# Retention and two gated MLP layers on one core: dense products of the first weight blocks dealt over the units of retention in another way

## Chip, core and metric

One core of a Trainium2 chip runs the whole kernel. The metric is the device time of one execution in microseconds, as the median of several runs. The profile is one execution with the hardware profiler on.

## What is computed

Retention over 2 x 8 heads (sequence 768, head size 64), then two MLP layers on its output x (1536 tokens by 512), all in fp32:

```python
state = gamma * state + einsum('bhd,bhe->bhde', k[:, :, t], v[:, :, t])
y[:, :, t] = scale * einsum('bhd,bhde->bhe', q[:, :, t], state)
...
x = ((x @ w_a) * (x @ w_b)) @ moe_w_out        # 512 -> 1536 -> 512
h = x @ w_in                                   # 512 -> 2048
y = np.maximum(0.01 * h, h) @ moe2_w_out       # 2048 -> 512
```

## The kernel before

**Precision.** TensorE runs the dense products in fp32r. Each fp32 operand is split in a high part (a ScalarE copy that rounds, names ending in h) and a low part (source minus high part, on VectorE, names ending in l), and a product is three matmuls: high by high, high by low, low by high (`mm3`, L256 to L258). Weights come from HBM as 64-bit words (`raw_...`, L286). For each block three ScalarE instructions take the word apart (`begin_steps`, L307, L309, L311) and three VectorE instructions round it (`round_steps`: L325, L327 and L329); then `high` (L944) and `low` (L950) split it.

**Retention** comes first. The 1536 tokens are 3 tiles of 512 and the 8 heads 4 pairs: 12 units (tile by tile, 4 pairs in each), driven by the loop over `u` at L1005. Units 0 to 3 use chunks of 128 tokens, units 4 to 11 short chunks of 64. For a short-chunk unit TensorE makes the states (`kv`, from scaled keys `kd` and `v`), the scores (`sc`), the part within a chunk (`x` from `P` and `v`) and the part across chunks (`x` from `qs` and the running states `cr`, `ca`). In iteration u it issues states(u+1) between within(u), then scores(u+1) between across(u), all at L644. The other engines then serve the next iteration:

- VectorE: seven or eight updates of the running state (`adds`, L606 and L608), `P` of unit u+1 (`masked`, L650), the low part of x (L251), and rounding and low parts of weights;
- ScalarE: scaled keys (L583), the high part of x (L250), plain or negated copies of x (`xf`, L663 and L665), the weights' first steps and high parts;
- GpSimd: scaled queries `qs` of later units (L588), each when its `q` has landed, and later its own DMAs.

Every engine works through its instructions in the program's order. The tiles are held in a pool of 83 slots of SBUF; a new tile waits for what last used its slot. PSUM has 8 banks, one for each of kv, sc, x and each open dense product.

**The dense products of blocks 0 and 1** of the first layer (a and b, three tiles of x: 48 steps of three 512-column matmuls) fill TensorE between the small products. The generator `first_blocks` (L953) lists them, and the loop takes `FILL[u]` steps at the end of iteration u, the rest after the last unit (L1089). A name such as pa01 or h01 has the tile first and the block second; tile n of the loop is stored under TURN[n]. `ROUND` says in which units a block is rounded (`weigh`): a and b of block 0 in units 3 and 4, those of block 1 in units 5 to 8, in two parts each. `PUMP[u]` takes items from a queue, among them block 2's rounding (from u = 8).

**After retention**, blocks 2 to 11 run in a scheme that needs fewer products but sums of x's quarters. The sums (`outer`, L1077) are eight accumulating DMAs on `xf` from GpSimd's queue, two in each of units 8 to 11; each half of them is a chain of four, in which one waits for the landing of the one before. `mixed_items` then splits eight of these sums into high and low parts (L760, L763), four queue items in each of units 9 to 11. Block 2's first matmul is `pa` from x10h and a2h.

```python
for _ in range(FILL.get(u, 0)):
    next(dense)
pump(PUMP.get(u, 0))
```

Of the kernel before, what the change touches and what calls it, by code (L numbers as in the profile page):

```python
# [10 lines left out]
F32R = mybir.dt.float32r  # L11
# [15 lines left out]
NPAIR = H // 2  # L27
# [8 lines left out]
NRAW = 4  # L36
NEXTRA = 10
NWARM = 10
FILL = {4: 4, 5: 4, 6: 4, 7: 4, 8: 4, 9: 4, 10: 4, 11: 4}
PUMP = {9: 0.6, 10: 0.6, 11: 0.6}  # L40
ROUND = {3: ("a", 0, 3), 4: ("b", 0, 3), 5: ("a", 1, 2), 6: ("a", 1, 1), 7: ("b", 1, 2), 8: ("b", 1, 1)}
NBLOCK = 2
AHEAD = 8
KEYS = {-1: (2,), 0: (3,), 3: (5,)}
QUERIES = {4: (6,), 5: (7, 8), 6: (9, 10), 7: (11,)}
CPT = TT // P
COUNT = {"a": FF1, "b": FF1, "wo": FF1, "wi": FF2, "wq": FF2}
HALF = FF2 // 2
# [180 lines left out]
def retention_moe_kernel(ctx: ExitStack, tc: tile.TileContext, ins, out):  # L229
# [14 lines left out]
    def as32(t):  # L244
        return t.bitcast(F32)

    def split(src, name, new=slots.new):

        hi, lo = new(F32R, name + "h"), new(F32R, name + "l")
        nc.scalar.copy(hi, src)  # L250
        nc.vector.tensor_sub(lo, src, as32(hi))  # L251
        return hi, lo
# [120 lines left out]
    def enqueue_split(key, keep=False, far=False):  # L373
        def high():
            weights[key] = slots.new(F32R, f"{key[0]}{key[1]}h"), slots.new(F32R, f"{key[0]}{key[1]}l")
            (nc.vector.tensor_copy if key[0] == "wi" and key[1] > 1 else nc.scalar.copy)(weights[key][0], rounded[key])

        def low():
            src = rounded.pop(key)
            if far:  # L380
                nc.scalar.mul(weights[key][1], as32(weights[key][0]), -1.0)
                nc.gpsimd.dma_start(weights[key][1], src, accum_op=ALU.add)
            else:
                nc.vector.tensor_sub(weights[key][1], src, as32(weights[key][0]))
            if keep:
                kept[key] = src
            else:
                slots.done(1)

        behind.extend([(0.05, high), (0.05 if far else 0.61, low)])  # L390

    def enqueue_next(f):
        for k in "ab":
            enqueue_round()
            enqueue_split((k, f), f in FAST, k == "a" and f in FAST[1:])

    kept = {}

# [160 lines left out]
    @known  # L559
    def wide_spreads(u, t, p, d):  # L560
        for h, r in enumerate(flip):
            nc.scalar.copy(spread[u % 2][r, 1:, heads[h]], broad[u % 2][r, 1:])
# [84 lines left out]
    @known  # L647
    def masked(u, t, p, d):
        d["P"] = slots.new(F32, f"P{u}")
        nc.vector.tensor_mul(by_sub(d["P"]), by_sub(d["sc"]), pair_table(p, 1))  # L650

    @known
    def leave_x(u, n, p, d):
        t = TURN[n]
        x[t, p] = split(d["x"], f"x{t}{p}")

    @known
    def copy_x(u, n, p, d):
        t = TURN[n]
        if t != 1:  # L660
            xf[t, p] = slots.new(F32, f"xf{t}{p}")
            if t:
                nc.scalar.mul(xf[t, p], d["x"], -1.0)  # L663
            else:
                nc.scalar.copy(xf[t, p], d["x"])  # L665
        slots.done(6)
        del un[u]
# [73 lines left out]

    S, yf, SY = {}, {}, {}

    def mixed_items(xf, S, name, summed=False):
        add, sub = nc.vector.tensor_add, nc.vector.tensor_sub
        for j in range(0 if summed else 2):
            for op, d, a, b in (
                (add, (2, 2 + j), (2, j), (2, 2 + j)),
                (sub, (2, j), (0, j), (2, j)),
                (sub, (0, j), (2, 2 + j), (0, j)),  # L750
                (sub, (0, 2 + j), (0, 2 + j), (0, j)),
            ):
                yield 0.61, lambda op=op, d=d, a=a, b=b: op(xf[d], xf[a], xf[b])
        for n, t, p in ((1, 2, 2), (3, 2, 0), (2, 0, 0), (4, 0, 2)):
            for j in range(2):
                key = (t, p + j)

                def high(n=n, key=key, j=j):
                    S[n, j] = slots.new(F32R, f"{name}{n}{j}h"), slots.new(F32R, f"{name}{n}{j}l")
                    nc.scalar.copy(S[n, j][0], xf[key])  # L760

                def low(n=n, key=key, j=j):
                    nc.vector.tensor_sub(S[n, j][1], xf.pop(key), as32(S[n, j][0]))  # L763
                    slots.done(1)

                yield 0.05, high
                yield 0.61, low
# [179 lines left out]
    def low():  # L947
        while lows:
            key = lows.pop()
            nc.vector.tensor_sub(weights[key][1], rounded.pop(key), as32(weights[key][0]))  # L950
            slots.done(1)

    def first_blocks():  # L953
        ps = {}
        all4 = range(KC)
        runs = [(0, 0, "a", all4), (0, 0, "b", all4)]
        runs += [(1, 0, k, kcs) for kcs in ((0, 1), (2,)) for k in "ab"] + [(0, 1, "a", (0, 1))]
        runs += [(1, 0, k, (3,)) for k in "ab"] + [(0, 1, "a", (2, 3)), (1, 1, "a", all4)]
        runs += [(n, 1, "b", all4) for n in range(2)]
        runs += [(2, f, k, all4) for f in range(2) for k in "ab"]  # L960
        for n, f, k, kcs in runs:
            t = TURN[n]
            for kc in kcs:
                if not kc:
                    ps[t, f, k] = bank(f"p{k}{t}{f}")
                ab_mm(ps[t, f, k], t, f, "ab".index(k), [kc])
                if kc == KC - 1 and k == "b":
                    ab_out(ps[t, f, "a"], ps[t, f, "b"], t, f)
                yield
# [4 lines left out]
    def keys(u):  # L974
        (wide_keys if u < NPAIR else scaled_keys)(u)

    def queries(u):
        (wide_queries if u < NPAIR else scaled_queries)(u)
# [5 lines left out]
    def rounding(u):  # L984
        weigh(u)
        if ROUND.get(u + 1, (0, 0, 0))[2] > 1:
            begin_weights()
        while done:
            high(done.pop())
# [15 lines left out]
    for u in range(-1, len(units)):  # L1005
        if u < NPAIR:
            if u < NPAIR - 1:
                wide_scores(u + 1)
            else:
                wide_within(u)  # L1010
                issue(states(u + 1))
                issue(scores(u + 1))
            if u < 0:
                keys(1)
                queries(1)
                keep_warm(3)
            if u == 0:
                wide_within(u)
            if u < NPAIR - 1:
                wide_states(u + 1)  # L1020
            else:
                masked(u + 1)
                for step in un[u + 1]["adds"]:
                    step()
            if u < 0:
                keep_warm(2)
            if 0 < u < NPAIR - 1:
                wide_within(u)
            wide_across(u)
            if u == NPAIR - 2:  # L1030
                keys(NPAIR)
                queries(NPAIR)
            leave_x(u)
            if u < NPAIR - 1:
                wide_spreads(u + 1)
            for v in KEYS.get(u, ()):
                keys(v)
                queries(v)
            copy_x(u)
            slots.tick()  # L1040
            rounding(u)
        else:
            issue(states(u + 1), within(u))
            issue(scores(u + 1), across(u))
            slots.tick()
            steps = un[u + 1]["adds"] if u + 1 in un else []
            low()
            for step in steps[:3]:
                step()
            masked(u + 1)  # L1050
            for step in steps[3:4]:
                step()
            keys(u + 2)
            for v in QUERIES.get(u, ()):
                queries(v)
            leave_x(u)
            for step in steps[4:]:
                step()
            rounding(u)
            copy_x(u)  # L1060
        for _ in range(FILL.get(u, 0)):
            next(dense)
        pump(PUMP.get(u, 0))
        loads(u + AHEAD)
        if u in (10, 11):
            load_weights()
        if u == 8:
            enqueue_next(2)
            queue.extend(behind)
            behind.clear()  # L1070
            queue.extend(sub_items(("a", 2), ("b", 2)))
        if u == 8:
            outer = [(xf[d], xf[a]) for d, a in outer]
        if u >= 8:
            for _ in range(2):
                d, a = outer.pop(0)
                nc.gpsimd.dma_start(d, a, accum_op=ALU.add)  # L1077
        if u == 8:
            spare.extend(mixed_items(xf, S, "s", True))
        for _ in range(4 if u > 8 else 0):  # L1080
            spare.pop(0)[1]()
        slots.tick()
    att.close()
# [437 lines left out]
```

## Time and profile before

| | us |
|---|---|
| median of 3 runs (lowest, highest) | 561.6 (561.35, 561.87) |
| the profiled execution | 561.61 |
| its span, first to last instruction | 559.8 |
| TensorE busy | 549.6 (98%) |
| VectorE busy | 461.5 (82%) |
| ScalarE busy | 385.4 (69%) |
| GpSimd busy | 154.9 (28%) |
| mean granted TensorE clock | 0.999 |

The profile calls TensorE PE, VectorE DVE, ScalarE ACT and GpSimd POOL. A row of the timeline has the start and the length of an instruction in us, the engine, the line, what is written from what, shapes, and in brackets how long the engine sat idle before it and what ended that. Matmuls overlap, and their ends are modelled: the distance between two starts says more than a length. Tile numbers are left out, so "pa<-x00h,a0h" is tile 0 and block 0.

### The profile page before, as it was taken

What the parts mean: (1) busy time and instruction counts of PE and PEld (TensorE: products, weight loads), DVE (VectorE), ACT (ScalarE), POOL (GpSimd) and SP (SyncE); (2) the same over time, 40 slices, a digit from 0 to 9 for tenths busy, and PEclk for the clock granted to TensorE, in tenths of its full rate; (3) what the DMA queues carried; (4) which work ended last, traced back from release to release, by engine and by line L of the source; (5) the groups of instructions that cost most, each with busy time, mean ns of one, the idle gap of its engine ahead of it and who ended that gap; (6) DMA issues with size and microseconds to landing.
All of it is one profiled execution on the core that took longest, in us unless ns stands there. A gap on an engine that the chain in (4) does not pass through costs nothing.

```text
span 559.8 us, 10494 instructions
## 1 busy us (share of the span) xinstructions
PE 549.6 (98%) x3745; PEld 462.3 (83%) x3745; DVE 461.5 (82%) x985; ACT 385.4 (69%) x795; POOL 154.9 (28%) x197
## 2 busy tenths in 40 slices
PE   9799999999999999999999999999999999999997
PEld 5777888888888888888888888888888888888886
DVE  5797887789998898999869878896977798999862
ACT  4864767678888888877757556778766886687800
POOL 2254101003213321267430130221333456600000
PEclk9999999999999999999999999999999999999999
DMA  8998614448887889699993361764777799964111
GB/s 316 395 385 232 151 42 117 127 119 228 238 233 206 249 229 299 200 326 232 247 218 96 58 131 42 213 179 151 227 239 224 209 274 241 224 163 118 57 57 57
DMA packets 49909, 108.52 MB, mean 194 GB/s; under 512 B 5952, under 2 KB 13376, under 8 KB 49856
## 3 DMA queue, kind: packets, MB, share of 16 engines
q1 hardware_dynamic: 27504, 66.86, 35.9%
q0 software_dynamic: 22064, 40.64, 34.0%
q8 instruction: 29, 0.48, 0.4%
q10 hardware_dynamic: 288, 0.34, 0.2%
q14 instruction: 24, 0.20, 0.1%
HBM read 74.00 MB, written 18.35 MB: 165 GB/s over the span
## 4 chain that ended last, share of the span: by engine, by line
PE 96%; DVE 2%; ACT 1%; issue 0%
PE blk L257 12%; PE blk L256 12%; PE blk L258 12%; PE top L257 5%; PE top L256 5%; PE top L258 5%; PE pa L256 4%; PE pb L258 4%; PE pb L256 4%; PE pb L257 4%; PE pa L257 4%; PE pa L258 4%; PE mid L256 3%; PE mid L257 3%; PE mid L258 3%; PE left L257 1%
## 5 line engine op out<-in xcount | busy, mean ns | idle before, releaser
L257 PE MATMUL blk<-form,form 128*128 128x512 f32 (+1 forms) x224 | 75.8, 339 | 0.0
L256 PE MATMUL blk<-form,form 128*128 128x512 f32 (+1 forms) x224 | 75.6, 337 | 0.0
L258 PE MATMUL blk<-form,form 128*128 128x512 f32 (+1 forms) x224 | 75.3, 336 | 0.0
L172 DVE TENSOR_TENSOR form<-g,form 128x512 fp32r<-128x512 f32 x112 | 57.5, 549 | 0.9
L257 PE MATMUL blk<-forma,forma 128*128 128x512 f32 (+1 forms) x168 | 56.9, 338 | 0.0
L256 PE MATMUL blk<-forma,forma 128*128 128x512 f32 (+1 forms) x168 | 56.7, 337 | 0.0
L258 PE MATMUL blk<-forma,forma 128*128 128x512 f32 (+1 forms) x168 | 56.4, 336 | 0.0
L166 ACT CAST form<-g 128x512 fp32r<-128x512 f32 x112 | 52.3, 511 | 5.1 <-DMA g<-g 3.2
L172 DVE TENSOR_TENSOR forma<-h,forma 128x512 fp32r<-128x512 f32 x84 | 43.0, 551 | 5.3 <-ACT forma L166 3.8
L256 PEld LDWEIGHTS blk<-form,form 128*128 128x128 f32 x224 | 42.5, 190 | 5.3
L257 PEld LDWEIGHTS blk<-form,form 128*128 128x128 f32 x224 | 42.5, 190 | 4.7
L258 PEld LDWEIGHTS blk<-form,form 128*128 128x128 f32 x224 | 42.3, 189 | 4.8
L166 ACT CAST forma<-h 128x512 fp32r<-128x512 f32 x84 | 38.8, 511 | 6.3 <-DMA h<-h 6.0
L717 POOL DMA_DIRECT2D farg<-g x26 | 15.6, 614 | 80.4 <-ACT g L1263 62.5
L145 POOL DMA_DIRECT2D h<-h x33 | 32.8, 1159 | 16.9 <-DVE h L847 5.1
L256 PEld LDWEIGHTS blk<-forma,forma 128*128 128x128 f32 x168 | 31.9, 190 | 4.0
L257 PEld LDWEIGHTS blk<-forma,forma 128*128 128x128 f32 x168 | 31.9, 190 | 3.6
L258 PEld LDWEIGHTS blk<-forma,forma 128*128 128x128 f32 x168 | 31.7, 189 | 3.6
L717 POOL DMA_DIRECT2D farh<-h x19 | 10.9, 575 | 75.4 <-DVE h L847 40.6
L172 DVE TENSOR_TENSOR form<-wq,form 128x256 fp32r<-128x256 f32 x56 | 23.3, 417 | 10.0 <-ACT form L166 9.9
L166 ACT CAST form<-wq 128x256 fp32r<-128x256 f32 x56 | 22.5, 402 | 6.4 <-PE blk L257 2.5
L145 POOL DMA_DIRECT2D g<-farg x22 | 22.0, 1046 | 7.9 <-DVE form L172 4.4
(3058 smaller groups left out, 1680.4 us busy)
## 6 DMA issues: line engine op xcount, KB each, us to landing
raw_wi<-in_w SPq DMA_DIRECT2D x16, 512.0 KB, 4.2
raw_wq<-in_w SPq DMA_DIRECT2D x16, 512.0 KB, 5.1
farg<-g POOLq DMA_DIRECT2D x26, 256.0 KB, 4.0
g<-farg SPq DMA_DIRECT2D x26, 256.0 KB, 6.7
raw_a<-in_wab SPq DMA_DIRECT2D x12, 512.0 KB, 5.0
raw_b<-in_wab SPq DMA_DIRECT2D x12, 512.0 KB, 5.0
raw_wo<-in_wo SPq DMA_DIRECT2D x12, 512.0 KB, 5.2
g<-farg POOLq DMA_DIRECT2D x20, 256.0 KB, 8.5
```

What stands on the lines that cost most here:

```text
L145: queue.append((0.0, lambda piece=piece: self.nc.gpsimd.dma_start(self.A(*d[1:], j)[piece], self.A(*x1[1:], j)[piece], accum_op=ALU.add)))
L166: nc.scalar.copy(h, src)
L172: nc.vector.tensor_sub(*todo.pop(0))
L256: nc.tensor.matmul(ps, w[0], x[0], start=first, stop=False, skip_group_check=more)
L257: nc.tensor.matmul(ps, w[0], x[1], start=False, stop=False, skip_group_check=more)
L258: nc.tensor.matmul(ps, w[1], x[0], start=False, stop=last, skip_group_check=more)
L717: nc.gpsimd.dma_start(self.far[t, f], self.tiles[t, f])
```

## The change

Steps are dealt as 4, then 6 in each of units 5 to 10, then 4, with 4 left after the last unit (before: 4 in each of units 4 to 11, 16 left). In `first_blocks` the products of block 0 with the second tile stay open over units 5 to 8, one quarter of x in each. Block 1's a and b are rounded in one unit each, 5 and 6. In units 3 and 4 rounding moves ahead of the state updates (unit 3) and of `P` (unit 4), and the high and low parts of a0 and b0 are made in that unit. Block 2's rounding and first sums are queued at u = 6 instead of 8, and PUMP takes them from u = 7. The low part of a2 and of the sums 3 and 4 (four tiles) is no longer a VectorE subtraction but a ScalarE multiplication by -1 and an accumulating DMA from GpSimd's queue. The eight `outer` sums are issued in units 8 and 9, four in each.

```diff
-FILL = {4: 4, 5: 4, 6: 4, 7: 4, 8: 4, 9: 4, 10: 4, 11: 4}
-PUMP = {9: 0.6, 10: 0.6, 11: 0.6}
-ROUND = {3: ("a", 0, 3), 4: ("b", 0, 3), 5: ("a", 1, 2), 6: ("a", 1, 1), 7: ("b", 1, 2), 8: ("b", 1, 1)}
+FILL = {4: 4, 5: 6, 6: 6, 7: 6, 8: 6, 9: 6, 10: 6, 11: 4}
+PUMP = {7: 1.2, 8: 1.6, 9: 1.2, 10: 1.2, 11: 1.2}
+ROUND = {3: ("a", 0, 3), 4: ("b", 0, 3), 5: ("a", 1, 3), 6: ("b", 1, 3)}
+LATER = {9: 4, 10: 6, 11: 6}
...
-            enqueue_split((k, f), f in FAST, k == "a" and f in FAST[1:])
+            enqueue_split((k, f), f in FAST, k == "a")
...
-                    nc.vector.tensor_sub(S[n, j][1], xf.pop(key), as32(S[n, j][0]))
+                    if n in far:
+                        nc.scalar.mul(S[n, j][1], as32(S[n, j][0]), -1.0)
+                        nc.gpsimd.dma_start(S[n, j][1], xf.pop(key), accum_op=ALU.add)
+                    else:
+                        nc.vector.tensor_sub(S[n, j][1], xf.pop(key), as32(S[n, j][0]))
...
                 masked(u + 1)
-                for step in un[u + 1]["adds"]:
+                weigh(u)
+                for step in un[u + 1]["adds"][:3]:
                     step()
...
+            if u == NPAIR - 1:
+                high(done.pop())
+                low()
+                for step in un[u + 1]["adds"][3:]:
+                    step()
+                x_low(u)
+                begin_weights()
...
+            if u == NPAIR:
+                weigh(u)
+                masked(u + 1)
+                for step in steps:
+                    step()
+                x_high(u)
+                keys(u + 2)
+                queries(u + 2)
+                high(done.pop())
+                low()
+                x_low(u)
+                begin_weights()
...
-        if u >= 8:
-            for _ in range(2):
+        if u in (8, 9):
+            for _ in range(4):
                 d, a = outer.pop(0)
                 nc.gpsimd.dma_start(d, a, accum_op=ALU.add)
         if u == 8:
-            spare.extend(mixed_items(xf, S, "s", True))
-        for _ in range(4 if u > 8 else 0):
+            spare.extend(mixed_items(xf, S, "s", True, (3, 4)))
+        for _ in range(min(LATER.get(u, 0), len(spare))):
```

**VectorE in iterations 3 and 4**, from the updates of unit 4 to b0's rounding, before. (cr0, cr1 and ca.. are running states, kv4 is unit 4's new states, sl the weight's low bits.)

```order
L251 TENSOR_TENSOR x03l_75_478<-x3_421,x03h_74_477 128x512
L325 TENSOR_SCALAR a0_68_408<-a0_68_408 128x512
L327 TENSOR_SCALAR a0_68_408<-a0_68_408 128x512
L329 ISA a0_68_408<-a0_68_408,sl0_409 128x1024
L950 TENSOR_TENSOR a0l_81_498<-a0_68_408,a0h_80_497 128x512
L608 SCALAR_TENSOR_TENSOR cr1_86<-ca11_80,second_76,kv5_508 128x64
L608 SCALAR_TENSOR_TENSOR cr1_86<-cr1_86,second_76,kv5_508 128x64 x2
L650 TENSOR_TENSOR P5_86_575<-sc5_540,second_76 128x512
L606 COPY cr1_86<-kv5_508 128x64
L251 TENSOR_TENSOR x20l_90_583<-x4_509,x20h_89_582 128x512
L608 SCALAR_TENSOR_TENSOR cr1_86<-cr1_86,second_76,kv5_508 128x64 x2
L608 SCALAR_TENSOR_TENSOR ca10_79<-cr1_86,second_76,kv5_508 128x64
```

And now:

```order
L965 TENSOR_TENSOR a0l_79_486<-a0_68_408,a0h_78_485 128x512
L607 COPY cr0_85<-kv4_430 128x64
L609 SCALAR_TENSOR_TENSOR cr0_85<-cr0_85,second_76,kv4_430 128x64 x2
L609 SCALAR_TENSOR_TENSOR ca00_77<-cr0_85,second_76,kv4_430 128x64
L662 TENSOR_TENSOR x03l_75_479<-x3_421,x03h_74_478 128x512
L326 TENSOR_SCALAR b0_80_494<-b0_80_494 128x512
L328 TENSOR_SCALAR b0_80_494<-b0_80_494 128x512
L330 ISA b0_80_494<-b0_80_494,sl1_495 128x1024
L651 TENSOR_TENSOR P5_86_577<-sc5_541,second_76 128x512
L609 SCALAR_TENSOR_TENSOR cr1_86<-ca11_80,second_76,kv5_509 128x64
```

a0's three rounding steps stand ahead of the rows shown, a0l among the updates of unit 4, and b0's steps ahead of P5 and of unit 5's updates, where they followed both.

**VectorE in iteration 5 and at the start of 6**, now: the rounding of a1, block 0's product h00 and a1's low part.

```order
L609 SCALAR_TENSOR_TENSOR ca20_81<-cr0_85,second_76,kv6_618 128x64
L326 TENSOR_SCALAR a1_93_598<-a1_93_598 128x512
L328 TENSOR_SCALAR a1_93_598<-a1_93_598 128x512
L330 ISA a1_93_598<-a1_93_598,sl2_599 128x1024
L700 TENSOR_TENSOR h00_105_728<-h00_105_728,pb00_715 128x512
L965 TENSOR_TENSOR a1l_103_711<-a1_93_598,a1h_102_710 128x512
L609 SCALAR_TENSOR_TENSOR cr1_86<-ca31_84,second_76,kv7_739 128x64
```

The same stretch before:

```order
L608 SCALAR_TENSOR_TENSOR ca20_81<-cr0_85,second_76,kv6_617 128x64
L325 TENSOR_SCALAR a1_91_594<-a1_91_594 128x512
L327 TENSOR_SCALAR a1_91_594<-a1_91_594 128x512
L689 TENSOR_TENSOR h00_102_717<-h00_102_717,pb00_704 128x512
L608 SCALAR_TENSOR_TENSOR cr1_86<-ca31_84,second_76,kv7_720 128x64
L608 SCALAR_TENSOR_TENSOR cr1_86<-cr1_86,second_76,kv7_720 128x64 x2
```

a1's third step (ISA) now follows at once, and h00's product stands between it and a1l; before, the third step came an iteration later.

**GpSimd after the last scaled queries**, before:

```order
L588 TENSOR_TENSOR qs11_115_901<-q11_84_504,second_76 128x512
L1077 DMA xf22_112_813<-xf20_94_602 128x512
L1077 DMA xf23_118_912<-xf21_101_702 128x512
L1077 DMA xf20_94_602<-xf00_47_286 128x512
L1077 DMA xf21_101_702<-xf01_56_344 128x512
L1077 DMA xf00_47_286<-xf22_112_813 128x512
```

And now:

```order
L589 TENSOR_TENSOR qs11_117_923<-q11_84_505,second_76 128x512
L383 DMA a2l_130_1075<-a2_122_956 128x512
L1116 DMA xf22_114_830<-xf20_94_603 128x512
L1116 DMA xf23_120_932<-xf21_104_713 128x512
L1116 DMA xf20_94_603<-xf00_47_286 128x512
L1116 DMA xf21_104_713<-xf01_56_344 128x512
```

The accumulating DMA of a2's low part stands ahead of all sums of xf; the low parts of four sums (s30l to s41l) follow the eighth.

## Rows read from the trace of the kernel before

**Rows 1.** The page's first part: busy us, share of span and instructions of each engine.

```profile
PE 549.6 (98%) x3745; PEld 462.3 (83%) x3745; DVE 461.5 (82%) x985; ACT 385.4 (69%) x795; POOL 154.9 (28%) x197
```

**Rows 2.** Waits of TensorE over the whole span: total us, times, longest.

```profile
PE kv L644 <- ACT kd L583: 1.6, 1, 1.6
PE x L644 <- issue: 1.1, 1, 1.1
PE pa L256 <- ACT a0h L944: 1.0, 1, 1.0
```

**Rows 3.** TensorE in order of time (start, length, engine, line, operation).

```profile
26.65 0.28 PE L644 MATMUL sc<-qs,k 64*64 64x64 f32 x4
...
27.96 0.50 PE L256 MATMUL pa<-x00h,a0h 128*128 128x512 f32 x1 [1.02 <-ACT a0h L944]
...
31.18 0.27 PE L644 MATMUL kv<-v,kd 64*64 64x64 f32 x2
...
37.33 0.27 PE L644 MATMUL kv<-v,kd 64*64 64x64 f32 x2
...
55.70 0.50 PE L256 MATMUL pa<-x20h,a1h 128*128 128x512 f32 x1
...
58.65 0.27 PE L644 MATMUL kv<-v,kd 64*64 64x64 f32 x2
...
60.67 0.50 PE L256 MATMUL pb<-x00h,b1h 128*128 128x512 f32 x1
...
68.49 0.39 PE L256 MATMUL pa<-x10h,a0h 128*128 128x512 f32 x1
...
79.37 0.39 PE L256 MATMUL pa<-x10h,a2h 128*128 128x512 f32 x1
```

**Rows 4.** GpSimd in order of time, units 5 to 9's scaled queries.

```profile
24.45 1.28 POOL L588 TENSOR_TENSOR qs<-q,second 128x512 f32<-128x512 f32 x1 [3.94 <-DMA q<-in_qT]
...
28.50 1.29 POOL L588 TENSOR_TENSOR qs<-q,second 128x512 f32<-128x512 f32 x1 [2.77 <-DMA q<-in_qT]
...
32.48 1.78 POOL L588 TENSOR_TENSOR qs<-q,second 128x512 f32<-128x512 f32 x1 [2.68 <-DVE b L327]
...
37.84 1.42 POOL L588 TENSOR_TENSOR qs<-q,second 128x512 f32<-128x512 f32 x1 [1.38 <-DVE ca L608]
```

**Rows 5.** VectorE in order of time, iterations 3 to 6.

```profile
22.37 0.27 DVE L608 SCALAR_TENSOR_TENSOR cr<-ca,second,kv 128x64 f32<-128x64 f32 x1
...
24.27 0.68 DVE L251 TENSOR_TENSOR x03l<-x,x03h 128x512 fp32r<-128x512 f32 x1
...
24.87 1.14 DVE L325 TENSOR_SCALAR a<-a 128x512 f32<-128x512 f32 x1
...
26.05 0.43 DVE L327 TENSOR_SCALAR a<-a 128x512 int32<-128x512 int32 x1
...
33.81 0.99 DVE L950 TENSOR_TENSOR b0l<-b,b0h 128x512 fp32r<-128x512 f32 x1 [0.68 <-ACT b0h L944]
...
38.15 1.39 DVE L327 TENSOR_SCALAR a<-a 128x512 int32<-128x512 int32 x1
```

**Rows 6.** ScalarE in order of time: a key, copies, then block 3's six steps.

```profile
23.38 0.72 ACT L583 ACTIVATE kd<-n,second 128x512 f32<-128x512 f32 x1
...
36.99 0.60 ACT L663 ACTIVATE xf<-x 128x512 f32<-128x512 f32 x1 [1.63 <-DVE x21l L251]
...
37.49 0.58 ACT L682 COPY h<-pa 128x512 f32<-128x512 f32 x1
...
78.56 0.69 ACT L307 ACTIVATE a<-raw_a 128x512 f32<-128x512 f32 x1
...
82.29 0.59 ACT L857 COPY h<-top 128x512 f32<-128x512 f32 x1
```

**Rows 7.** The instructions of line L1077, the sums of xf (ns min/median/max).

```profile
L1077 POOL DMA_DIRECT2D xf<-xf x8: 851/860/1009, 46.2 to 61.1; - x8
...
DMA to landing us min/median/max: 3.5/3.9/5.6
```

More of the change, by code (lines that the diff above doesn't have):

```diff
@@ L38 @@
 NWARM = 10
-FILL = {4: 4, 5: 4, 6: 4, 7: 4, 8: 4, 9: 4, 10: 4, 11: 4}
-PUMP = {9: 0.6, 10: 0.6, 11: 0.6}
-ROUND = {3: ("a", 0, 3), 4: ("b", 0, 3), 5: ("a", 1, 2), 6: ("a", 1, 1), 7: ("b", 1, 2), 8: ("b", 1, 1)}
+FILL = {4: 4, 5: 6, 6: 6, 7: 6, 8: 6, 9: 6, 10: 6, 11: 4}
+PUMP = {7: 1.2, 8: 1.6, 9: 1.2, 10: 1.2, 11: 1.2}
+ROUND = {3: ("a", 0, 3), 4: ("b", 0, 3), 5: ("a", 1, 3), 6: ("b", 1, 3)}
 NBLOCK = 2
+LATER = {9: 4, 10: 6, 11: 6}
 AHEAD = 8
 KEYS = {-1: (2,), 0: (3,), 3: (5,)}
-QUERIES = {4: (6,), 5: (7, 8), 6: (9, 10), 7: (11,)}
+QUERIES = {5: (7, 8), 6: (9, 10), 7: (11,)}
 CPT = TT // P
@@ L652, in leave_x, with x_high, x_low @@
     @known
-    def leave_x(u, n, p, d):
+    def x_high(u, n, p, d):
         t = TURN[n]
-        x[t, p] = split(d["x"], f"x{t}{p}")
+        x[t, p] = slots.new(F32R, f"x{t}{p}h"), slots.new(F32R, f"x{t}{p}l")
+        nc.scalar.copy(x[t, p][0], d["x"])
+    @known
+    def x_low(u, n, p, d):
+        hi, lo = x[TURN[n], p]
+        nc.vector.tensor_sub(lo, d["x"], as32(hi))
+    def leave_x(u):
+        x_high(u)
+        x_low(u)
     @known
@@ L742, in retention_moe_kernel, with mixed_items @@
     S, yf, SY = {}, {}, {}
-    def mixed_items(xf, S, name, summed=False):
+    def mixed_items(xf, S, name, summed=False, far=()):
         add, sub = nc.vector.tensor_add, nc.vector.tensor_sub
@@ L955, in first_blocks @@
         all4 = range(KC)
[L956 to L960, printed above, removed]
+        runs = [(0, 0, "a", all4), (0, 0, "b", all4)] + [(1, 0, k, (0,)) for k in "ab"]
+        for kc, k in ((1, "a"), (2, "b")):
+            runs += [(1, 0, k2, (kc,)) for k2 in "ab"] + [(0, 1, k, all4)]
+        runs += [(1, 0, k, (3,)) for k in "ab"] + [(1, 1, k, all4) for k in "ab"]
+        runs += [(2, 0, k, (kc,)) for kc in range(2) for k in "ab"] + [(2, 1, k, (0, 1)) for k in "ab"]
+        runs += [(2, f, k, (kc,)) for kc in (2, 3) for f in range(2) for k in "ab"]
         for n, f, k, kcs in runs:
@@ L1032, in retention_moe_kernel @@
                 queries(NPAIR)
-            leave_x(u)
+            x_high(u)
             if u < NPAIR - 1:
+                x_low(u)
                 wide_spreads(u + 1)
@@ L1038, in retention_moe_kernel @@
                 queries(v)
+            if u == NPAIR - 1:
[3 more added lines that the diff above has]
+                    step()
+                x_low(u)
+                begin_weights()
             copy_x(u)
             slots.tick()
-            rounding(u)
+            if u < NPAIR - 1:
+                rounding(u)
         else:
@@ L1046, in retention_moe_kernel @@
             steps = un[u + 1]["adds"] if u + 1 in un else []
[L1047 to L1059, printed above, removed]
+            if u == NPAIR:
[3 more added lines that the diff above has]
+                    step()
+                x_high(u)
+                keys(u + 2)
+                queries(u + 2)
+                high(done.pop())
+                low()
+                x_low(u)
+                begin_weights()
+            else:
+                low()
+                for step in steps[:3]:
+                    step()
+                masked(u + 1)
+                for step in steps[3:4]:
+                    step()
+                keys(u + 2)
+                for v in QUERIES.get(u, ()):
+                    queries(v)
+                leave_x(u)
+                for step in steps[4:]:
+                    step()
+                rounding(u)
             copy_x(u)
@@ L1066, in retention_moe_kernel @@
             load_weights()
-        if u == 8:
+        if u == 6:
             enqueue_next(2)
```

## Prediction

> **What bounds the kernel now.** I read the page's head first: TensorE is busy for 549.6 us, 98% of the span [rows 1], so a change that leaves its matmuls as they are can win at most the 10 us in which it has nothing to do. The waits of TensorE come next, to see where those lie: the longest are for a scaled key (kd, 1.6 us), for a small product's operand ("issue", 1.1) and for a0h (1.0) [rows 2]. Third, TensorE in order of time, where a reader should measure start to start, because a matmul's recorded end is modelled. An undisturbed fill of four dense steps lasts 2.95 us (55.70 to 58.65), the small products of a unit after it 2.02 (58.65 to 60.67) [rows 3]. Against these two numbers the stretch after 26.93, where unit 5's scores end, shows what is lost: the first fill starts at 27.96 instead of 26.93 and lasts 3.22 (1.3 us lost); from 31.18 to 37.33 a unit and a fill take 6.15 instead of 4.97 (1.2); the "issue" wait costs 1.1 and about 0.2 to start again; some 0.2 is spread over the other units. That is 4.0 us, and no more can come out of the change: the wait for kd, earlier, stays, since ScalarE does the same work ahead of it in both orders. From 51 us to the last block TensorE has no gap, so whatever block 2 gains at its first matmul (79.37 now [rows 3]) arrives at the end.
>
> Last I read GpSimd, VectorE and ScalarE in the same stretch, for what would be late next. GpSimd scales the queries (qs, 1.28 us each) at the moment each load lands, at 24.45, 28.50, 32.48 and 37.84 among others [rows 4]. Whenever a VectorE instruction with no operand in PSUM comes in that time, it is held to the end of the GpSimd one: L325 at 24.87 takes 1.14 us instead of about 0.42, L327 at 38.15 takes 1.39 where the same line at 26.05 takes 0.43, b0l at 33.81 takes 0.99 [rows 5]. They end 0.28 us (L325, L327) or 0.54 us (b0l) after the GpSimd instruction. x03l at 24.27, which reads PSUM, is not held [rows 5].
>
> **The change, step by step,** in the clock of the trace before.
>
> *Block 0's a, rounded before the state updates.* VectorE is free at 22.37, after P4. Three rounding steps (two shifts of 0.45 each, L327's 0.43 with its start, and a full-width step of 0.6, the distance from x03l at 24.27 to the next instruction) end at 23.9, three of the seven updates (1.90 us for all [rows 5]) at 24.75. ScalarE makes kd from 23.38 and then a0h, ready at 24.6 [rows 6]. So a0l is due at 24.75, three microseconds earlier than now, but qs5 has started at 24.45. a0l ends at 26.27 by the pattern of b0l. The four other updates follow, the last state that unit 4's products need is there at 27.1, where TensorE would have read it at 26.5. The first fill starts at 27.4: the wait for a0h (1.3 with the slow first fill) goes, and 0.45 comes in its place.
>
> *Block 0's b, rounded in one unit, ahead of P5.* After x03l (0.60) VectorE starts b0's steps at 27.88, 28.33 and 28.78. qs6 comes at 28.50, gets the port when the second step ends, and holds the third to 30.4. P5 is written at 31.05. TensorE, done with its fill at 27.4 + 2.95 = 30.35, waits 0.7 for P5. In the old order P5 stood ahead of the rounding and nothing on TensorE hung on it. Then seven updates (1.90) end at 32.86, b0l meets qs7 (32.48 to 33.76) and ends at 34.3. TensorE finished the unit at 33.05 and wants b0l for its third matmul at 33.6: 0.7 and 0.1 to start again. The two old losses here (1.2) are replaced by 1.5.
>
> *Block 1's a in one unit, its low half behind h00.* x20l (34.8), three updates and P6 bring VectorE to 36.3; x21l waits for ScalarE, which after x20l still makes xf20, kd7 and x21h (36.6); three more updates end at 38.07. a1's first step meets qs9 (37.84, to about 39.1 [rows 4]) and the rounding ends at 40.5 instead of 39.6. The product for h00 now stands ahead of a1l on VectorE, and on ScalarE a1h, xf21 and h00 come one after the other at 0.5 us each (xf at 36.99, h at 37.49 [rows 6]): h00 at 42.15, its product 0.6, a1l 0.6, ready at 43.5. TensorE, with six steps to a fill (2.95 + 1.36), wants a1l at 42.0: 1.5 lost and 0.1 to start again.
>
> *The rest.* The 1.3 around the old "issue" wait (a scaled key queued on ScalarE behind xf) goes: with six steps in each fill the key has 4.3 us instead of 2.95. From there on I find margins only: b1l at 49.4 for a matmul at 49.9, kd10 at 57.2 for 58.8, P11 at 69.1 for 71.4. Five subtractions leave VectorE (0.6 us each). Five ScalarE multiplications and five GpSimd DMAs (0.86 us of issue, as each xf sum [rows 7]) take their place, a2's ahead of the eight xf sums in GpSimd's queue. I price them at nothing, because TensorE wants their products later. a2l's multiplication comes at 59.1 (x23l ends at 51.7; then on ScalarE xf23 and h01, six rounding steps for a2 and b2, kd10, x10h, h20, a2h, a2l; six such steps take 3.7 us, from 78.56 to 82.29 [rows 6]). The first xf sum starts at 60.05. After three stages of 4.05, s20h and with it x13h and x13l are there at 75.5, for a matmul at 76.6. After four, at 77.3, ScalarE has s41 (1.0), four half copies (1.1), six steps (3.7) and h02 (0.5) to do: 83.65, for a matmul into that bank at 79.0 + 24 x 0.227 = 84.4 (0.227 is 68.49 to 79.37 by its 48 matmuls [rows 3]). What it costs without that cover is the third rival.
>
> **Sum.** Removed 1.3 + 1.2 + 1.3 + 0.2 = 4.0; new 0.45 + 0.7 + 0.8 + 1.6 = 3.55, rounded to 3.6. Net 0.4 us earlier: 561.6 - 0.4 = **561.2 us**. The profiled execution (561.61) lies 0.01 from the median of the runs, so the sum stands for both. Bounds: nothing new waits (4.0 less), or every new wait is 0.3 longer than worked out (about 0.8 more). I take the middle because each hold rests on a landing time that this trace shows, and the loads' order does not change. A difference under 0.2% (1.1 us) I call no change.
>
> On the holds, this trace shows three of them on VectorE, and one on GpSimd (qs7 takes 1.78 [rows 4], with a rounding step ahead of it). The Trainium skill (SBUF — State Buffer, "Who interferes with whom") says of such instructions (two SBUF inputs, or a two-port mode) that whoever issues first keeps the port for the whole instruction. By that rule alone the third step of b0 could also win. By the rows GpSimd takes the port in the gap between two VectorE steps, as with L327 at 38.15.
>
> **Rivals.**
> 1. *The rounding slips through.* If the third step of b0 begins before qs6, P5 is ready by 30.1, b0l at 32.6 comes just ahead of qs7 or loses little, and a1's rounding ends at 37.9, with a1l at 40.7 for a matmul at 40.4. New waits: 0.45 + 0 + 0 + 0.4, gain about 3.1: **558.5**. For it: 0.3 us decide, and the landing of q6 is one sample. Against: VectorE's steps from 26.27 to 28.50 are all of measured length.
> 2. *Only the last hold fails.* If qs9 and a1's rounding miss each other, the wait for a1l shrinks from 1.6 to 0.6: **560.2**. For it: five landings and many steps lie ahead of that meeting. Against: a 1.28 us window on a 1.5 us job.
> 3. *The sums come late (slower).* GpSimd issues in order. It now issues a2's accumulating DMA first, which waits for ScalarE's a2l at 59.1, where the xf sums now start at 46.2 [rows 7]. Four of them follow one another, each after the landing of the one before (3.5 to 5.6 us, median 3.9 [rows 7]), and ScalarE stands waiting for the last with a3, b3 and h02 behind. Up to 4.2 us a stage nothing is lost. At 5.0 h02 is 3.8 later and TensorE stops for 3: **564.2**. Against: few other transfers are left at that time. The Trainium skill (SBUF — State Buffer, "SBUF: two separate sides") tells of GpSimd's DMA going from 620 to 3100 ns beside a VectorE copy. An estimate from that page is 11 us more, near 573. The trace does not agree: the eight issues took 0.85 to 1.01 us [rows 7], with VectorE at work 82% of the span [rows 1].
>
> **Numbers.** The forecast has 0.52, rival 1 0.20, rival 2 0.18, rival 3 0.10. The forecast's own range is 560.4 to 562.0. To leave out no more than 2 in 10 the range reaches over rival 2 and rival 1 with half a microsecond on its far side, and as much past the forecast's upper bound: 558.0 to 562.5. Faster: rivals 1 and 2 and 0.05 of the forecast, 0.43. Slower: rival 3 and 0.02 of the forecast, 0.12. The same: 0.45.
>
> **What would show it.** Right: a0l, b0's third step and b0l each about 1 us long or more beside a qs; waits of TensorE for P5, b0l and a1l, and none for a0h, b0h or the old "issue"; the first pa of block 2 (a2h) at about 79.0. A first matmul of block 2 at 76 to 77 and no wait for P5 would show rival 1. Wrong: a wait of TensorE after 50 us (for x13l, h02 or a bank), or block 2 starting after 79.4.

## The result, and the profile after

The changed kernel takes 564.4 us (median of 10 runs, 562.95 to 566.63), the kernel before 561.6 on the same chip (10 runs, 561.12 to 562.45): a ratio of 1.0052, 95% interval 1.0037 to 1.0067. It is slower by 2.8 us, where 561.2 was forecast. The profiled execution took 564.86, its span is 563.1.

The page's first part, after:

```profile
PE 553.0 (98%) x3745; PEld 463.3 (82%) x3745; DVE 459.0 (82%) x980; ACT 388.9 (69%) x800; POOL 158.8 (28%) x202
```

VectorE has five instructions fewer and ScalarE and GpSimd five more each [rows 1], as the change says. The waits of TensorE, in the columns of [rows 2]:

```profile
PE top L257 <- ACT h L872: 1.4, 1, 1.4
PE kv L645 <- ACT kd L584: 1.4, 1, 1.4
PE warm L942 <- DVE warm L933: 1.2, 1, 1.2
PE pa L259 <- DVE a1l L965: 1.1, 1, 1.1
PE sc L533 <- DMA k<-in_kT: 0.6, 1, 0.6
PE x L645 <- DVE cr L607: 0.4, 1, 0.4
PE top L257 <- ACT h L876: 0.2, 1, 0.2
```

The waits for a0h and "issue" are gone, a1l's is there. Of the new rows, the first and the last lie in block 2: h02 (L872) and h22 (L876) are copies that empty a PSUM bank, and the next matmul into that bank waits for them. TensorE in order of time:

```profile
25.88 0.28 PE L645 MATMUL kv<-v,kd 64*64 64x64 f32 x2 [1.37 <-ACT kd L584]
...
79.96 0.39 PE L257 MATMUL pa<-x10h,a2h 128*128 128x512 f32 x1
...
86.94 0.50 PE L257 MATMUL top<-s20h,tb2h 128*128 128x512 f32 x1 [1.38 <-ACT h L872]
...
95.66 0.50 PE L257 MATMUL top<-x22h,ta2h 128*128 128x512 f32 x1 [0.24 <-ACT h L876]
```

These rows cut the kernel in two stretches that compare well: from unit 5's first state (kv, the one that waits for the scaled key kd) to block 2's first pa, and from there to the end of the span. After: 79.96 - 25.88 = 54.1 and 563.1 - 79.96 = 483.1. Before: 55.2 and 480.4 (the 79.37 of [rows 3], and the span in the table of before; unit 5's first kv came at 24.15 there). So the first stretch, which holds the new dealing, is 1.1 shorter here. (Of the profiles below that keep this dealing, two that also started late have 0.6 and 1.3, and the five that started at 23.7 to 24.3 have 0.1 to 0.4, three of them with the granted clock at 0.50 for 3.4 to 6.8 us from 25 or 26 on.) And 2.7 us are lost behind block 2's start. By the starts of the matmuls against before, 1.5 of them lie at the wait for h02, 0.4 at that for h22, 0.4 at 102.87 in block 3, where the timeline gives no wait, and the rest in small steps. Together with a start 1.7 later that makes the 3.3 us between the two profiled executions. GpSimd shows where the 2.7 come from:

```profile
60.38 1.05 POOL L383 DMA_DIRECT2D a2l<-a  x1 [13.95 <-ACT a2l L382]
61.09 2.13 POOL L1116 DMA_DIRECT2D xf<-xf  x2
...
66.56 0.85 POOL L1116 DMA_DIRECT2D xf<-xf  x1 [3.34 <-DMA xf<-xf]
...
77.05 0.86 POOL L1116 DMA_DIRECT2D xf<-xf  x1 [1.55 <-DMA xf<-xf]
```

GpSimd stands for 14 us for ScalarE's a2l, with the first xf sum behind it; the sums run from 61.1 to 77.1 where they ran from 46.2 to 61.1 [rows 7]. ScalarE, in order of time:

```profile
80.42 0.62 ACT L771 CAST s41h<-xf 128x512 fp32r<-128x512 f32 x1 [0.45 <-DMA xf<-xf]
...
82.67 0.68 ACT L308 ACTIVATE a<-raw_a 128x512 f32<-128x512 f32 x1
...
86.31 0.58 ACT L872 COPY h<-top 128x512 f32<-128x512 f32 x1
```

It gets the last sum at 80.42; its multiplication, four half copies and six rounding steps follow, and h02 comes at 86.31, where TensorE had ended at 85.56. That is the mechanism of the third rival.

### The profile page after: what moved, and what is told of

Read it like the earlier page. It is cut to its first block, busy times and chain, and to the rows that moved or that the text cites. A ratio compares the mean times of both kernels' runs of the same rounds, so it can differ in the third digit from the quotient of the medians.

```text
span 563.1 us, 10494 instructions
## 1 busy us (share of the span) xinstructions
PE 553.0 (98%) x3745; PEld 463.3 (82%) x3745; DVE 459.0 (82%) x980; ACT 388.9 (69%) x800; POOL 158.8 (28%) x202
## 4 chain that ended last, share of the span: by engine, by line
PE 81%; DMA 9%; ACT 5%; DVE 3%; issue 1%; POOL 0%; SPq 0%; ACTq 0%; POOLq 0%
PE blk L258 12%; PE blk L257 12%; PE blk L259 12%; PE top L257 5%; PE top L258 5%; PE top L259 5%; DMA xf<-xf 3%; PE mid L257 3%; PE mid L259 3%; PE mid L258 3%; PE pb L259 2%; PE pb L257 2%; PE pb L258 2%; PE pa L259 2%; PE pa L257 2%; PE pa L258 2%
```

## The experiments

All medians below stand against the kernel before, timed beside them on the same chip. That kernel took 561.6 us beside the changed kernel and 562.3, 562.5 and 561.9 in the three later comparisons, so kernels are compared by their ratios. "To block 2" and "to the end" are the two stretches, from one profile each.

| kernel | median us (runs) | ratio to before, 95% | to block 2 | to the end |
|---|---|---|---|---|
| before | 561.6 (10) | 1 | 55.2 | 480.4 |
| changed | 564.4 (10) | 1.0052 (1.0037 to 1.0067) | 54.1 | 483.1 |
| after_again | 564.5 (9) | 1.0047 (1.0031 to 1.0062) | 55.1 | 485.2 |
| sums_first | 569.2 (4) | 1.0132 (1.0113 to 1.0150) | 62.3 | 483.1 |
| a2_near | 561.9 (12) | 0.9990 (0.9980 to 1.0000) | 54.9 | 480.6 |
| a2_between | 561.3 (12) | 0.9978 (0.9968 to 0.9987) | 55.1 | 480.6 |
| s_near | 563.2 (12) | 1.0018 (1.0002 to 1.0033) | 54.9 | 484.4 |
| both_near | 561.4 (12) | 0.9987 (0.9971 to 1.0003) | 53.9 | 480.5 |
| early_only | 570.4 (4) | 1.0147 (1.0132 to 1.0161) | 55.0 | 489.9 |
| h02_first | 564.9 (11) | 1.0051 (1.0033 to 1.0069) | 54.6 | 484.2 |
| a1l_first | 561.4 (12) | 0.9984 (0.9973 to 0.9995) | 54.5 | 481.6 |
| best1 | 559.4 (6) | 0.9950 (0.9935 to 0.9965) | 53.0 | 480.5 |
| best2 | 560.0 (12) | 0.9957 (0.9940 to 0.9974) | 53.3 | 480.5 |
| before_again | 564.0 (1) | none | 57.2 | 480.4 |

### The changed kernel again

> The changed kernel once more, for its head and its spread. Theory A (queue order): the loss is made after block 2 starts, because a2l's accumulating DMA stands ahead of the eight xf sums in GpSimd's queue; then TensorE waits again about 1.4 us for h02 (ScalarE, line 872), some 0.2 for h22, and from block 2's first pa to the end 2.7 us are lost against before, whatever the start was. Theory B (late start): the loss is the 1.7 us by which unit 4's scaled key came later; if that belongs to the kernel, TensorE gets it at 25.9 again, and if it was an accident of one execution it comes at 24.2 and the time is near 562.7. A forecasts 564.4 with a spread of runs as wide as the start varies.

Waits of TensorE:

```profile
PE top L257 <- ACT h L872: 3.1, 1, 3.1
...
PE pb L259 <- DVE b0l L965: 0.5, 1, 0.5
```

Unit 5's first state, which waits for the key, came at 23.76 this time, so the late start of the first profile belongs to single executions, and theory B falls: the start was early and the time no better. (A wait of 0.6 for the first k stood at the head of that profile; it recurs in h02_first.) The wait for h02 is longer still, 3.1, and 4.8 us are lost after block 2's start. The other 1.7 are mostly the clock. Behind the wait TensorE's granted clock stood at 0.50, its 1.2 GHz level, from 87.0 to 90.4, and matmuls started 0.43 us apart instead of 0.23; in the first profile, with a wait of 1.4, it stayed at 1.00. A stretch of 2 us (the number behind the last bracket is the clock):

```profile
88.00:90.00 2.00, 2.00 (x6) 1.54 (x6) 0.69 (x1) 1.73 (x5) 0.86 (x1) 0.50 0.80 229
```

A holds in its place, with larger sizes, and so does the forecast up to block 2: its first pa came at 78.84, for 79.0.

### Where a2's DMA stands on GpSimd's queue

Three kernels change this, a fourth is their counterpart, and none changes TensorE's instructions. First, all sums ahead:

```diff
+        if u == 8:
+            for d, a in outer:
+                nc.gpsimd.dma_start(xf[d], xf[a], accum_op=ALU.add)
         pump(PUMP.get(u, 0))
...
-        if u in (8, 9):
-            for _ in range(4):
-                d, a = outer.pop(0)
-                nc.gpsimd.dma_start(d, a, accum_op=ALU.add)
```

> The eight xf sums are put ahead of the queue items of unit 8, so that on GpSimd all eight stand before a2l's DMA; nothing else moves. Theory A: the first sum is issued at about 47 instead of 61, the last has landed by 66, ScalarE has s41h before 72, no wait of TensorE for h02 or h22, and the time falls by 2.7 to about 561.7 (lower still if the start is not late). Theory B (late start): no change, 564.4. Theory C (ScalarE's five added multiplications make h02 late, not the order): h02 still comes at about 86 and the time stays within 0.5 of 564.4.

It was 569.2, the worst but one. GpSimd and VectorE in order of time, then a wait of TensorE:

```profile
68.45 1.21 POOL L383 DMA_DIRECT2D a2l<-a  x1
```

```profile
73.37 0.42 DVE L406 TENSOR_TENSOR a<-a,b 128x256 f32<-128x256 f32 x1 [7.36 <-DMA a2l<-a]
```

```profile
PE x L645 <- DVE P L651: 5.2, 1, 5.2
```

The sums were issued from 50.0 to 67.9, early as A says (though not from 47), and h02 was not waited for (h22 was, for 1.2 in all). But now a2's DMA stood behind all eight of them and went out at 68.45, and L406, which overwrites the a2 that this DMA reads, stood on VectorE until it had landed at 73.4. Unit 11's P was behind L406, and TensorE behind P. Its granted clock then stood at 0.50 from 73.8 to 80.6, which made the matmuls behind the wait some 1.5 us later still. No theory had this wait. It is the same fault on the other side: an accumulating DMA that is waited for, behind others on one queue.

So the subtraction was put back for a2 alone:

```diff
-            enqueue_split((k, f), f in FAST, k == "a")
+            enqueue_split((k, f), f in FAST, k == "a" and f in FAST[1:])
```

> Only a2's low part goes back to a VectorE subtraction; its multiplication and DMA go, the four tiles of sums 3 and 4 stay on ScalarE and the DMA. Theory A: GpSimd has nothing ahead of the sums, the first is issued at about 47 and the time is 561.7 to 562 as with the sums ahead. Theory B: 564.4. Theory C: one of five multiplications is gone, 0.6 us less at h02: 563.8.

Measured 561.9, no wait after the one for a1l, 480.6 to the end, with the first sum issued at 49.6 (for 47). And then a2's DMA again, but issued between the fourth and the fifth sum:

> a2's low part again by the accumulating DMA, but on GpSimd's queue behind the first four xf sums and ahead of the last four. The first two orders each held something for it: ahead of all sums they came late (ScalarE's s41h at 80.4), behind all sums the DMA itself came late (issued at 68.5, and VectorE stood 7.4 us for it before it may overwrite a2). Theory A (only the place in the queue): the four sums are issued from 50 to 58, a2l at about 60, its landing at 65 to 66 costs VectorE under 1 us, the last sum has landed by 74, no wait for h02 or for unit 11's P; time as with a2 near, 562.0 within 0.5. Theory D (an accumulating DMA of a2 costs about 5 us wherever it stands): a wait of 1 to 5 us for P or for h02 remains and the time is above 563.

```diff
+        if u == 8:
+            for d, a in (outer.pop(0) for _ in range(4)):
+                nc.gpsimd.dma_start(xf[d], xf[a], accum_op=ALU.add)
         pump(PUMP.get(u, 0))
...
+        if u == 9:
+            for d, a in outer:
+                nc.gpsimd.dma_start(xf[d], xf[a], accum_op=ALU.add)
```

GpSimd and ScalarE of this kernel:

```profile
59.41 1.07 POOL L383 DMA_DIRECT2D a2l<-a  x1 [1.78 <-ACT a2l L382]
...
67.55 0.86 POOL L1116 DMA_DIRECT2D xf<-xf  x1 [0.41 <-DMA xf<-xf]
```

```profile
76.91 0.60 ACT L771 CAST s41h<-xf 128x512 fp32r<-128x512 f32 x1
...
82.78 0.59 ACT L872 COPY h<-top 128x512 f32<-128x512 f32 x1
```

561.3: the same instructions as the changed kernel, 3.1 us less (a ratio of 0.9978 for 1.0052), from the place of four sums in one queue. The last sum is issued at 67.6 instead of 77.1 (77.7 in after_again), s41h waits for none, h02 comes 3.5 earlier (4.2). Theory D falls: the DMA costs nothing that can be measured where nothing waits for it.

The counterpart puts sums 3 and 4 back and leaves a2 where the change has it:

```diff
-            spare.extend(mixed_items(xf, S, "s", True, (3, 4)))
+            spare.extend(mixed_items(xf, S, "s", True))
```

> The counterpart of a2_near: a2 stays on ScalarE and the DMA, ahead of the xf sums, and the four tiles of sums 3 and 4 go back to VectorE. Theory A: the sums still wait for a2l, s41h still comes at about 80, ScalarE is spared only the last multiplication (0.6), so TensorE waits 0.8 to 2.5 for h02 and the time is 563.8. Theory C (ScalarE's four added multiplications and the four DMAs): the wait for h02 goes and the time is 562.

```profile
80.38 0.62 ACT L771 CAST s41h<-xf 128x512 fp32r<-128x512 f32 x1 [1.90 <-DMA xf<-xf]
...
85.61 0.57 ACT L872 COPY h<-top 128x512 f32<-128x512 f32 x1
```

The wait for h02 stays, 2.0, and 4.0 us are lost to the end; some 1.7 of them go with a granted clock of 0.50 from 86.7 to 90.1. (This execution took 564.8, above its kernel's median.) Theory C falls as the whole cause: with four of the five multiplications gone the sums are as late. But the ratio is 1.0018 where the changed kernel had 1.0052 and 1.0047, some 1.8 us better, and A gave the move 0.6 (563.8, for a median of 563.2). What the other 1.2 are is not shown.

### Both halves apart

> All five low parts (a2, sums 3 and 4) back on VectorE; the new dealing and the earlier queue of block 2 stay. Theory A: the five subtractions (0.6 each) lie on VectorE where nothing on TensorE waits for them, so the move to ScalarE and GpSimd gains nothing: 561.9 within 0.6, as a2_near. If VectorE's load mattered, 1 to 3 us more than a2_near.

561.4, for 561.9 of a2_near (ratios 0.9987 and 0.9990): the five subtractions on VectorE cost nothing that can be measured, so moving them gained nothing.

> The new dealing of blocks 0 and 1 alone: a2 and the sums back on VectorE, block 2's rounding queued at u = 8, the sums two in each of units 8 to 11, pump and later items as before. Theory A: no wait after block 2's start, 561.5 (the middle gained 1.1 in the first profile, against a start that was 1.7 late: 560.5 if the start is as before). Theory B: still 563 to 564. Theory C: as A, since the multiplications are gone too.

No theory came true, since the run was badly cut. ScalarE, in order of time:

```profile
92.81 0.62 ACT L425 CAST tb3h<-b 128x512 fp32r<-128x512 f32 x1 [4.05 <-DVE b L412]
...
94.37 0.61 ACT L771 CAST s41h<-xf 128x512 fp32r<-128x512 f32 x1
94.89 0.58 ACT L855 COPY u<-top 128x512 f32<-128x512 f32 x1
```

The old dealing left 16 steps after the last unit, each with a pump of queued items; the new one leaves 4. With the old, late queue the splits of sum 4 had not been taken when block 2 began, they came behind block 3's tb3h, and TensorE stood 6.4 us for u (L855), then ran for 6.8 us at a granted clock of 0.50. To block 2 the kernel took 55.0, like the others. So the dealing needs the earlier queue of the same change, and this run says nothing about the cause.

### What stands behind the sums on ScalarE

> The changed kernel with the six first steps of a3's and b3's rounding behind h02 on ScalarE instead of ahead of it; a2's DMA is still ahead of the xf sums, so s41h still comes at 80 to 81. Theory A (the late sums push everything that ScalarE does behind them): h02 comes at about 83.4 and its wait goes, but a3's low part, which was issued at 88.4 and 89.0 in the two profiles of the changed kernel, comes 0.4 later, so tb3h, ta3h and h22 behind it come 3 us after TensorE wants h22 (93): the wait moves to h22, time 563.5 to 564.5. If h02's place on ScalarE were the whole trouble: no wait for h22 over 0.4, time 561.7.

```diff
-        else:
-            pump(2.0)
         if f == FAST[-1]:
```

Waits of TensorE:

```profile
PE top L257 <- ACT h L876: 1.7, 1, 1.7
...
PE top L257 <- ACT u L855: 0.9, 1, 0.9
```

564.9, 0.4 above A's range. The wait for h02 went and came back as 1.7 for h22 and 0.9 for u, both further down ScalarE's order. A had the whole of it at h22: the mechanism is right, the split was not. So h02 was only the first instruction that the late sums pushed.

### The three holds and a faster version

On top of a2_near, a1l moved ahead of h00's product, by one call behind the rounding of units 5 and up:

```diff
                 rounding(u)
+                low()
```

> On top of a2_near, a1's low part is written ahead of block 0's product h00 on VectorE instead of behind it. By the forecast's chain (a1h, xf21, h00 on ScalarE, then the product, then a1l) the wait of TensorE for a1l, 1.06 us in four of five profiles so far and 0 in none with this order, goes altogether: a1l ends near 41.9 for a matmul at 42.6. Time 560.8 (561.9 less 1.1). If instead qs9, which holds a1's first step, sets it, a wait of 0.3 to 0.6 stays and the time is 561.3.

The wait for a1l is gone, and the profile shows none of 0.3 to 0.6 in its place. But to block 2 the gain is 0.4 (54.5 for 54.9), and 0.9 is given back after it, 0.4 of it as a wait for h22; where the rest goes is not shown. The median against before (0.9984) cannot be told from a2_near's (0.9990).

Then x03l behind b0's three steps:

```diff
                 weigh(u)
+                hi, lo = x[TURN[0], NPAIR - 1]
+                nc.vector.tensor_sub(lo, x3, as32(hi))
                 masked(u + 1)
```

(with its old call taken out, and x3 kept there as the bank it reads.)

> On top of a1l_first, the low part of x03 moves from ahead of b0's three rounding steps to behind them, so that the third step begins at about 28.2, ahead of qs6 (28.5), instead of 28.9 behind its start. By the forecast's reading of the holds: the step takes 0.7 instead of 1.56, P5 is written by 30.1 and TensorE does not wait for it (0.45 in a2_near); b0l begins ahead of qs7 (32.5) and takes 0.7 instead of 1.47, and its wait (0.65) goes. Time 559.7. If VectorE is not held by GpSimd but late for its own work, P5 and b0l come no earlier and the time is that of a1l_first, 560.8.

VectorE and GpSimd, first in a2_near, then in best1:

```profile
28.53 1.38 POOL L589 TENSOR_TENSOR qs<-q,second 128x512 f32<-128x512 f32 x1 [2.80 <-DMA q<-in_qT]
28.90 1.56 DVE L330 CUSTOM_DVE_ANT_0 b<-b,sl 128x1024 uint16<-128x1024 uint16 x1
...
32.52 1.28 POOL L589 TENSOR_TENSOR qs<-q,second 128x512 f32<-128x512 f32 x1 [2.61 <-DMA q<-in_qT]
...
32.88 1.47 DVE L965 TENSOR_TENSOR b0l<-b,b0h 128x512 fp32r<-128x512 f32 x1
```

```profile
28.03 0.69 DVE L330 CUSTOM_DVE_ANT_0 b<-b,sl 128x1024 uint16<-128x1024 uint16 x1
28.24 1.65 POOL L589 TENSOR_TENSOR qs<-q,second 128x512 f32<-128x512 f32 x1 [2.77 <-DMA q<-in_qT]
...
32.03 0.69 DVE L965 TENSOR_TENSOR b0l<-b,b0h 128x512 fp32r<-128x512 f32 x1 [0.20 <-issue]
32.22 1.65 POOL L589 TENSOR_TENSOR qs<-q,second 128x512 f32<-128x512 f32 x1 [2.34 <-PE x L645]
```

559.4 (for 559.7), ratio 0.9950: faster than both kernels, with no wait for P5, b0l or a1l, and 1.9 us less to block 2 than a2_near. The meetings with qs6 and qs7 turned round: VectorE came first, kept its 0.69, and GpSimd took 1.65 instead of 1.28 to 1.38.

> a2's DMA between the fourth and the fifth xf sum, a1l ahead of h00's product, x03l behind b0's rounding steps. The gains of a2_between (561.3 against before's 562.5) and of the two moves on VectorE (1.9 us from kd5 to block 2's first pa in best1 against a2_near) should add: 559.0 to 559.4, no wait for P5, a0l, b0l, a1l, h02. If a2's subtraction on VectorE cost nothing, it is not faster than best1 (559.4).

560.0 (ratio 0.9957), above the 559.0 to 559.4 of the sum: no faster than best1, so a2's subtraction on VectorE costs nothing that can be measured here either.

> The kernel before once more, for the two stretches that the comparisons use: 55.2 us from unit 5's first kv (kd5) to block 2's first pa, 480.4 from there to the end of the span, both within 0.4 if the one profile so far is typical; a stop of TensorE of about 1.1 near 48 that the profile puts down to nothing (issue) again, if it belongs to the kernel.

This one execution took 564.0, and the second stretch was 480.4 again; the first was 57.2, so that expectation failed by 2.0. TensorE waited 1.67 for a0h and 0.80 for a0l, and its granted clock fell; stretches of 2 us, as above:

```profile
26.00:28.00 2.00, 0.96 (x60) 0.82 (x55) 1.16 (x3) 2.00 (x5) 0.00 (x0) 1.00 1.06 401
28.00:30.00 2.00, 0.99 (x2) 0.30 (x2) 1.39 (x1) 2.00 (x5) 1.28 (x1) 0.73 1.03 384
30.00:32.00 2.00, 1.58 (x4) 1.30 (x5) 1.93 (x7) 1.54 (x3) 0.00 (x0) 0.50 1.07 391
...
34.00:36.00 2.00, 2.00 (x47) 1.35 (x49) 1.25 (x4) 0.67 (x2) 0.79 (x1) 0.56 1.05 383
```

Its first fill took 6.36 (28.63 to 34.99) for 3.22 before.

## Why the prediction was wrong

**The step that failed** is in the paragraph "The rest": the five GpSimd DMAs "I price them at nothing, because TensorE wants their products later". The place was right, and so was the start: the first sum was put at 60.05 and was issued at 60.23 and 60.02 in after_again and s_near (61.09 in the first profile, which began late). What was mis-sized is the stage of the chain, "three stages of 4.05" and "After four, at 77.3": 17.25 us from the first issue to s41h, of which four stages are 16.2. It took 19.3, 20.9 and 20.4 us (changed, after_again, s_near). By the forecast's own count that is 4.6 to 5.0 a stage, and the point that I had named myself was 4.2. The rest of that sum held: 6.35 from s41h to the end of h02, measured 6.5 (80.42 to 86.89). The sign that I had named for it, a wait after 50 us for h02, is in both profiles of the changed kernel.

I had taken little more than the median of one landing (3.9) for a stage. In the trace of the changed kernel a stage is a landing and then 0.3 us (0.5 ahead of the last sum) to the next issue, and the landings were longer than before: a median of 4.2, 4.7 and 4.8 us in the three profiles. The longest of the first profile stand at the head. There a2l's DMA and the first two sums, issued within 1.3 us, landed at 65.0, 66.3 and 67.6, one after the other, so the second sum took 5.9. Why later landings were long too is not shown.

The same group of rows hinted at it: eight issues from 46.2 to 61.1 and a landing of 3.9 behind them [rows 7] are 18.8 us, and with that the forecast's own sum gives 60.05 + 18.8 + 6.35 = 85.2 for the matmul at 84.4. Not all of it is the chain, since the second sum of before stood 1.05 for a ScalarE copy:

```profile
48.30 0.90 POOL L1077 DMA_DIRECT2D xf<-xf  x1 [1.05 <-ACT xf L663]
```

Without that the sum is 84.1. So the rows gave the third rival a chance near one in two, not one in ten. Its mechanism is what happened, with stops of 1.4, 3.1 and 2.0 us where it had 3. That its price (564.2) lies so near the measured 564.4 is in part luck: it had neither the late start of some executions nor the lower clock behind the stop in others.

**The other steps.** The waits of the middle came where they were put, in profiles that started as before did. In a2_near: b0's third step 1.56 long beside qs6, P5 waited for 0.45 (0.7 forecast), b0l 0.65 (0.8), a1l 1.06 (1.6); the waits for a0h, b0h and "issue" were gone. In after_again the step took 1.56 and b0l 1.45, with a wait of 0.5 for b0l and none for P5. In the first profile of the changed kernel, which started late, they missed qs6 and qs7 and took 0.69 and 0.68, and TensorE waited for neither. The rounding was held by qs9 (its first step took 1.24 there), and a1l stood behind the product for h00 as said. Block 2's first pa came at 78.84 and 79.18 (79.0 forecast). With the late sums out of the way the time is what the sum said: a2_near's ratio is 0.9990 (0.9980 to 1.0000) for 561.2 / 561.6 = 0.9993. The terms are not all as near: the new waits for P5, b0l and a1l add up to 2.2 there, for 3.1 forecast, and TensorE's waits between the two marks fell by 1.1 in all, but the stretch by 0.3 only. Where the rest went is not shown, so some of the agreement is luck. Rival 1 did not happen by itself; best1, which moves a1l too, made it happen, and to block 2 it was worth 1.9 us of the 2.7 that the rival was given over the forecast. "Five subtractions leave VectorE" is worth nothing that can be measured (both_near). Rival 2 did not happen.

What I said of the "issue" wait, a scaled key queued on ScalarE behind xf, is not shown. Both profiles of before have a stop of about 1 us there (1.09 and 0.93) with no releaser, the changed kernel has none, and best1 has a stop of 0.86 at another place. The profile names a running state (cr) for it, which that matmul does not read, and its weight load had started at 46.77. Weight loads and then the matmul of best1:

```profile
46.77 0.19 PEld L259 LDWEIGHTS pb<-x00h,b1l 128*128 128x128 f32 x1 [0.32 <-DVE b1l L965]
47.73 0.19 PEld L257 LDWEIGHTS pb<-x01h,b1h 128*128 128x128 f32 x1 [0.77 <-issue]
```

```profile
47.73 0.39 PE L259 MATMUL pb<-x00h,b1l 128*128 128x512 f32 x1 [0.86 <-DVE cr L609]
```

Its cause stays open; no run was made for it.

## What to carry to other kernels

When a DMA moves onto a queue that works in order, look at the first thing behind it: a waiting DMA at the head costs what is late behind it, and one at the tail costs whoever waits for its landing. Here the same DMAs gave 569, 564 and 561 us by their order (with some 1.5 us of the lower clock in the 569). Price a chain of transfers by the whole chain's rows, first issue to last landing, not by its links times a median; and a rival whose decision point lies 4% beyond the value taken (4.2 for 4.05) has a chance near one in two, not one in ten.

## What the runs showed of the hardware

The holds between GpSimd and VectorE go both ways: the instruction that began second lost 0.8 to 0.9 us on VectorE (1.56 and 1.47 for 0.69) and about 0.3 on GpSimd (1.65 for 1.28 to 1.38), as one or the other came first by 0.2 to 0.4 us. The Trainium skill (SBUF — State Buffer, "Who interferes with whom") has whoever issues first keep the port; the rows of a2_near and best1 agree in both directions.

An accumulating DMA of 256 KB within SBUF took 3.3 to 5.9 us from issue to landing in the changed kernel (median 4.2). The Trainium skill (DMA: Bandwidth & Descriptors, "Anatomy of one DMA — SWDGE (gpsimd) path") gives about 2.0 us and the bytes at 436 GB/s for a DMA from GpSimd, an estimate of 2.6 for this size; for these accumulating DMAs the trace does not agree.

In before_again TensorE was busy for 0.96 and 0.99 us of two stretches of 2 us (26 to 30), with waits of 1.67 and 0.80, and its granted clock went to 0.50, the 1.2 GHz level, from 28.9 to 35.8. The first fill took 6.36 instead of 3.22, of which 0.80 is the wait for a0l. In the first profile of before the stretch from 26 to 28 looks the same (0.97), the wait for a0h was 1.0, there was none for a0l, and the clock stayed at 1.00 there. So 1.4 us more of waiting, and the lower clock behind it, went with a first stretch 2 us longer, once. A wait did not always bring the clock down: it stayed at 1.00 behind the 1.4 us for h02 in the changed kernel and fell to 0.50 for 3.4 us behind the 2.0 in s_near and the 3.1 in after_again.
